# Attention and routed experts: value products in bursts by a fixed table, constants built on the chip, halves swapped by a transfer

## The chip, the cores and the metric

One core of a Trainium2 chip runs the whole program. The metric is the device time of one execution in microseconds; the kernel before is shown with three runs and one profiled execution.

## The reference, cut to what matters

```python
def _attn_ref(q, k, v, tau):                      # q, k, v: (8, 8, 576, 64)
    scores = scale * np.matmul(q, k.transpose(0, 1, 3, 2))
    thresh = np.max(scores, axis=-1, keepdims=True) - tau
    scores = np.where(scores >= thresh, scores, -1000000000.0)
    scores = scores - np.max(scores, axis=-1, keepdims=True)
    attn = np.exp(scores)
    attn = attn / (np.sum(attn, axis=-1, keepdims=True) + 1e-09)
    return np.matmul(attn, v)
def _moe_ref(x, w_gate, w1, w2):                  # x: (4608, 512), 8 experts, F = 1024
    logits = x @ w_gate
    order = np.argsort(-logits.flatten())         # tokens in falling order of their logit,
    ...                                           # each expert takes at most 576
    for e in range(E): out[mask] = np.maximum(x[mask] @ w1[e], 0.0) @ w2[e]
```

## The kernel before, in words

**The attention loop.** Two heads make a pair, four pairs a batch, 32 pairs in all (NP). A pair has nine tiles of 128 queries (the ninth takes the last 64 queries of both heads), so there are NT = 288 tiles, and the loop `for s_ in range(-2,NT//2+2)` (L301) takes two of them in each slot. In slot s, TensorE (PE) issues in this order: the scores of two tiles that are two slots ahead (`score`, L70, into `sc`), a few transposes of leftover columns in some slots (`left`, into free columns of `sc`), value products and other units, and last the 16 transposes of the tiles of this slot (`tr`, L102, into `tb`). VectorE (DVE) does two row minima with a copy (`mx`, L78, the z instructions) and two threshold products (`stt`, L94). ScalarE (ACT) empties `tb` of the slot before (`trev`, L117 and L119, two instructions), takes two exponentials (`ex`, L90), and empties what the slot before has left in the value banks.

**Buffers that tie the engines.** `sc` has two buffers, one for each tile of a slot, so the scores of the next slot wait for the z of this one. `tb` has one buffer for both tiles, so the transposes of a slot wait until ACT has emptied those of the slot before. The value products use two PSUM banks, `xa` and `xb`.

**Value portions.** A pair's value product is nine units: four over the first 256 queries (`pv_unit(p,0,u)`, L154, bank `xa`), four over the other 320 (`pv_unit(p,1,u)`, bank `xb`) and one for the leftover keys (`pl_unit`, L169). One `pv_unit` is two matmuls in the program and four in the trace, since each fp32 matmul is recorded twice. In the kernel before, `push_pair` puts the units into a queue with conditions, and `columns(n=2)` takes two units in each slot as their conditions hold.

**Gates.** When a batch's four pairs are done, `finish` queues its units: two gate products (`lg_unit`, L190), their transposes (`lgt_unit`, L201, `lgm_unit`, L210), and for batches 0 and 1 five units that transpose the rows and store them (`xt_unit`, L222). `whole()` issues one of them in a slot if a bank is free, after the slot's value portions. The first gate product also holds a matmul with `swap` (L192) that brings the reciprocals of the other half of the partitions, which ACT then copies into `rm` (L197).

**Start and end.** Constants come as one array `cst` by a transfer on the POOL queue (`load_cst`, L946); `Router.consts` (L396) makes bf16 and fp32r copies from it on DVE before the first z. After the loop come the rest of the last pair, the gates of the last batch, and a search over thresholds (`R.phase`), with row transposes of the late batches between its steps. `R.prep(0,28)` and `R.compare` prepare that search for seven of eight batches. The expert part follows (`moe`); its order is set by a planner that keeps a model time of DVE, to which every DVE instruction of the router is added (`Vec`).

Of the kernel before, what the change touches and what calls it, by code (L numbers as in the profile page):

```python
# [9 lines left out]
F32 = mybir.dt.float32  # L10
# [12 lines left out]
def attention(ctx, tc, qk, vl, tau, wgd, xrows, xts, Lg, nb_batches, ident, swap, R, after_first):  # L23
# [154 lines left out]
    def rd_calc(b):  # L178
        rd=wk.tile([128,36],F32,name="rd",bufs=XTB+NBO); RD[b]=rd
        G.tensor_scalar(rd,DEN[b],1e-9,None,op0=ALU.add)  # L180
        V.reciprocal(rd,rd)
        rm=wk.tile([128,4,2],F32,name="rm",bufs=XTB+NBO); RD["m",b]=rm
        for h in range(2):
            r=slice(64*h,64*h+64); G.tensor_scalar(rm[r,:,h],rd[r,32:36],1.0,0.0,op0=ALU.mult,op1=ALU.add)
    LT={}
    def lg_unit(b,f):
        if f==0: LT[b]=wk.tile([128,S+D],F32,name="lt",bufs=LTB)
        ps=bank_g(b,[128,512]); q=FQ[f]; n=q.stop-q.start; rd=RD[b]
        for j in range(4):
            T.matmul(ps[32*j:32*j+32,:n],wg[:,j],XT[b][:,j,q],start=True,stop=True,tile_position=(0,32*j))  # L190
        if f==0:
            T.matmul(ps[:,256:260],swap,rd[:,32:36],start=True,stop=True)  # L192
        def ev():
            A.activation(LT[b][:,q],ps[:,:n],AF.Copy)
            if f==1: G.tensor_scalar(LT[b][:,S:],LT[b][:,S-D:S],1.0,0.0,op0=ALU.mult,op1=ALU.add); return
            for h in range(2):
                r=slice(64*h,64*h+64); A.activation(RD["m",b][r,:,1-h],ps[r,256:260],AF.Copy)  # L197
# [20 lines left out]
    def xt_unit(b,c):  # L218
# [7 lines left out]
        def ev():  # L226
            src=RD[b][:,8*c:8*c+8] if c<4 else RD["m",b][0:64].rearrange("p j h -> p (j h)")
            fv=xr[:n,512:XW]; xv=xr[:n,:512].rearrange("p (j d) -> p j d",j=4)
# [11 lines left out]
    queue=[]; aux=[]; later=[]; late=[]; late2=[]; st={"last":-9,"slot":0}  # L240
    def push_pair(p):
        b,j=divmod(p,4)
        def when(n): return lambda: have.get((p,n),1<<30)+HOLD<=st["slot"]
        def units(f): queue.extend(("c",when("t3" if f==0 else "t8"),lambda f=f,u=u: pv_unit(p,f,u),"ab"[f] if u==0 and (f==0 or late_p(p)) else None) for u in range(4))
        def note(w,g): queue.append(("n",w,g,None))
        units(0)
        if j==3: note(when("t8"),lambda: rd_calc(b))
        if p==NP-1:


            units(1)
            def left(f):
                for k,g in pl_unit(p,(f,)): g(); VB[k]["free"]=True
            for g in (lambda: left(0),lambda: left(1),lambda: lg_unit(b,0)(),lambda: lg_unit(b,1)(),lambda: lgt_unit(b)(),lambda: lgm_unit(b)()):
                note(when("pl"),g)
            note(lambda: not later,lambda: late.extend([lambda c=c: xt_unit(b,c) for c in range(5)]))
            return
        queue.append(("c",when("pl"),lambda: pl_unit(p),"b"))
        units(1)
        if (b,j)==(nb_batches-1,2): note(lambda: not aux,lambda: (R.prep(0,28),R.compare(R.k("E1"),J,0,28)))  # L260
        if j==3: note(lambda: not later,lambda: finish(b))
    def finish(b):
        aux.extend([(2,lambda: lg_unit(b,0)),(2,lambda: lg_unit(b,1)),(2,lambda: lgt_unit(b)),(2,lambda: lgm_unit(b))])
        rows=[lambda c=c: xt_unit(b,c) for c in range(5)]
        if nb_batches-NDEF-NBO<=b<nb_batches-NDEF:
            nc.sync.dma_start(xts[b],XT[b]); late2.extend(rows)
        elif b<nb_batches-NDEF: aux.extend([(1,x) for x in rows])
# [6 lines left out]
    def columns(n=2):  # L274
        while queue and queue[0][1]():
            k,_,g,bk=queue[0]
            if k=="c":
                if n==0: return
                if bk and not VB[bk]["free"]: return
                n-=1  # L280
            queue.pop(0); r=g()
            if k=="c" and r: later.extend(r)
# [685 lines left out]
```

## Time and profile before

| what | value |
|---|---|
| median of 3 runs | 991.3 us (991.24 to 991.8) |
| the profiled execution, its own time | 989.73 us |
| its span, first to last instruction | 988.0 us (1.73 us lie around it) |
| mean granted TensorE clock | 0.988 |
| busy: PE, DVE, ACT, POOL | 954.5, 769.8, 641.0, 224.7 us |

A busy PE is not a PE at its peak: the ends of matmuls are modelled, and the time between two starts says more than the length of one. The chain is the work that ended last, followed back from the end. An idle time in brackets stands before the instruction that it delayed.

### The profile page before, as it was taken

Reading aid. Unit: us, or ns where it says so; the run is one execution under the profiler, and the core shown is the slowest. Engines: PE = TensorE matmul, PEld = TensorE weight load, DVE = VectorE, ACT = ScalarE, POOL = GpSimd, SP = SyncE. Lnnn points to the kernel's source line nnn. Section 1 sums busy time; section 2 is a strip of 40 time slices with the busy share of each in tenths; the row PEclk is TensorE's granted clock in tenths of the full one; section 3 lists DMA queues with packets and bytes.
Section 4 is the critical chain, followed back from the end, with each engine's and each line's share of the span. In section 5 each row is a group of like instructions: output and inputs, shape, how many; then the busy total and the mean of one; then the engine's idle time right before and its main releaser. Section 6 shows DMA issues by size and latency. Waiting matters only on the chain.

```text
span 988.0 us, 23677 instructions
## 1 busy us (share of the span) xinstructions
PE 954.5 (97%) x9141; PEld 707.4 (72%) x9141; DVE 769.8 (78%) x2100; ACT 641.0 (65%) x1283; POOL 224.7 (23%) x292
## 2 busy tenths in 40 slices
PE   6999999999999999999779999999999999999996
PEld 3566556555665566555679798897988979898994
DVE  6999999999999999997579878687787786535220
ACT  4999998999999998987645344253452534545340
POOL 2222322323222222222020313221302213310202
PEclk8999999999999999999979999999999999999998
DMA  6233241452432323303760705243433435341101
GB/s 233 96 107 121 103 157 55 169 182 88 169 122 98 121 90 117 121 2 121 268 222 2 245 28 181 93 136 112 141 122 113 145 108 166 100 149 41 38 12 42
DMA packets 35792, 116.97 MB, mean 118 GB/s; under 512 B 4384, under 2 KB 5024, under 8 KB 35168
## 3 DMA queue, kind: packets, MB, share of 16 engines
q1 hardware_dynamic: 28208, 92.58, 27.4%
q0 software_dynamic: 5968, 19.29, 6.2%
q10 hardware_dynamic: 1504, 3.59, 1.2%
q8 instruction: 72, 1.18, 0.5%
q14 instruction: 40, 0.33, 0.1%
HBM read 93.01 MB, written 21.38 MB: 116 GB/s over the span
## 4 chain that ended last, share of the span: by engine, by line
PE 90%; DVE 4%; DMA 2%; issue 2%; ACT 1%; ACTq 0%; POOLq 0%; POOL 0%; DVEq 0%
PE pf L798 21%; PE pf L830 19%; PE sc L70 15%; PE tb L102 9%; PE xb L154 8%; PE xa L154 6%; PE pt L743 2%; PE xa L169 1%; PE rps L451 1%; PE sc L102 1%; DMA out_dram<-y,idx 1%; PE xa L222 1%; DMA cst<-cst_dram 1%; DMA w1s<-w_dram 1%; DVE cmp L383 1%
## 5 line engine op out<-in xcount | busy, mean ns | idle before, releaser
L78 DVE TENSOR_SCALAR_CACHE_REDUCE z<-sc 128x576 f32<-128x576 f32 x288 | 205.6, 750 | 18.0 <-PE sc L70 16.0
L90 ACT ACTIVATE pp<-z,nb 128x576 f32<-128x576 f32 x256 | 193.2, 773 | 32.8 <-DVE z L78 31.1
L94 DVE SCALAR_TENSOR_TENSOR pp<-z,nb,pp 128x576 f32<-128x576 f32 x256 | 199.7, 812 | 0.0
L830 PE MATMUL pf<-w2h,H 128*128 128x512 f32 x576 | 195.1, 402 | 0.7 <-DVE H L383 0.7
L70 PE MATMUL sc<-qk 64*128 64x288 f32 (+1 forms) x1280 | 180.8, 427 | 5.8 <-DVE z L78 5.4
L79 POOL TENSOR_SCALAR nb<-nb,taub 128x2 f32<-128x2 f32 x144 | 105.9, 736 | 320.5 <-ACT pp L90 166.6
L117 ACT ACTIVATE pt<-tb 128x512 f32<-128x512 f32 x256 | 139.3, 590 | 5.3 <-PE tb L102 4.8
L830 PE MATMUL pf<-w2l,H 128*128 128x512 f32 x320 | 128.3, 401 | 0.0
L830 PEld LDWEIGHTS pf<-w2h,H 128*128 128x128 f32 x576 | 106.5, 189 | 19.9 <-DVE H L383 1.5
L70 PEld LDWEIGHTS sc<-qk 64*128 64x128 f32 (+1 forms) x1280 | 94.4, 180 | 35.4 <-DVE z L78 8.7
L102 PEld LDWEIGHTS tb<-ident,pp 64*128 64x128 f32 x2048 | 75.5, 139 | 54.1 <-issue 23.6
L837 POOL DMA_INDIRECT out_dram<-y,idx x40 | 43.8, 1095 | 305.9 <-ACT y L833 239.1
L798 PE MATMUL pf<-xh,w1h 128*128 128x288 f32 (+2 forms) x512 | 110.1, 301 | 0.7 <-ACT xh L744 0.7
L798 PE MATMUL pf<-xl,w1h 128*128 128x288 f32 (+2 forms) x512 | 110.1, 301 | 0.0
L798 PE MATMUL pf<-xh,w1l 128*128 128x288 f32 (+2 forms) x512 | 109.5, 299 | 0.0
L833 ACT ACTIVATE y<-pf 128x512 f32<-128x512 f32 x40 | 23.9, 598 | 127.5 <-PE pf L830 124.1
L102 PE MATMUL tb<-ident,pp 64*128 64x64 f32 x2048 | 94.1, 229 | 2.6 <-ACT pt L117 2.6
L810 ACT ACTIVATE hf<-pf 128x576 f32<-128x576 f32 x56 | 36.5, 653 | 89.5 <-PE pf L798 82.8
L154 PE MATMUL xb<-pt,vt 128*64 128x320 f32 x512 | 86.3, 448 | 0.0
L798 PEld LDWEIGHTS pf<-xh,w1h 128*128 128x128 f32 x512 | 82.0, 190 | 1.5 <-ACT xh L744 1.1
L798 PEld LDWEIGHTS pf<-xl,w1h 128*128 128x128 f32 x512 | 82.0, 190 | 0.0
L798 PEld LDWEIGHTS pf<-xh,w1l 128*128 128x128 f32 x512 | 81.8, 189 | 0.1
(214 smaller groups left out, 1398.4 us busy)
## 6 DMA issues: line engine op xcount, KB each, us to landing
qk<-qk_dram SPq DMA_DIRECT2D x31, 864.0 KB, 4.7
vt<-vl_dram SPq DMA_DIRECT2D x32, 576.0 KB, 3.8
w2s<-w_dram SPq DMA_DIRECT2D x32, 512.0 KB, 4.4
w1s<-w_dram SPq DMA_DIRECT2D x28, 512.0 KB, 5.7
xrows<-pp SPq DMA_DIRECT2D x24, 260.0 KB, 2.2
xts<-xt SPq DMA_DIRECT2D x2, 1152.0 KB, 5.2
pt<-xts SPq DMA_DIRECT2D x2, 1152.0 KB, 7.4
xrows<-xr SPq DMA_DIRECT2D x8, 260.0 KB, 2.4
```

Of the source, the lines that this page charges most:

```text
L70: T.matmul(sc[o,f,:HS], kd["q",h][r,c], kd["k",h][r,:],start=True,stop=True)
L78: V.tensor_scalar(z,SC.pop(t)[:,:,:HS],-0.125,None,op0=ALU.mult,op1=ALU.min,accum_out=nb[:,0,t%2:t%2+1])
L79: G.tensor_scalar(nb[:,1],nb[:,0],taub[:,0:1],None,op0=ALU.add)
L90: A.activation(pview(t),ZB[t].rearrange("p a b -> p (a b)"),AF.Exp,bias=NBI[t][:,0:1],scale=-1.0)
L94: V.scalar_tensor_tensor(pv,ZB.pop(t).rearrange("p a b -> p (a b)"),NBI[t][:,1:2],pv,op0=ALU.is_le,op1=ALU.mult,accum_out=den_of(p)[:,dcol ...
L102: g=slice(64*r,64*r+64); T.transpose(o[:,r],x[r%len(x)][g],ident[g,g])
L117: A.activation(PT[p][:,i%2,:,(i//2)*128:(i//2+1)*128].rearrange("p k (r q) -> p r k q",r=2),tb,AF.Copy)
L154: T.matmul(xo[64*h:64*h+64,:q.stop-q.start],v[:,f,128*u+64*h:128*u+64*h+64],PT[p][:,h,u,q],start=opens,stop=closes,skip_group_check=True)
L798: T.matmul(ps[:,h,:n],s[w][:,k,f*128:(f+1)*128],s[x][:,k,cols[h]],start=(i==0),stop=(i==11))
L810: A.activation(hf,ps[:,:,:HS],AF.Relu)
L830: T.matmul(ps[:,0,:],H[:,f,c:c+128],s[w][:,f],start=(f==0 and j==0),stop=e)
L837: G.indirect_dma_start(out=out,out_offset=IOA(ap=s["idx"][:n,t:t+1],axis=0),in_=y[:n],in_offset=None)
```

## The change

Value portions follow a table: in each round of nine slots (two pairs), slots 4, 6, 8, 1 and 3 (counted modulo 9) get 4, 4, 4, 4 and 2 units, and the others none. The gate condition reads `plan.get(slot)` after `columns()` has taken the slot's entry out. The `swap` matmul and its two ACT copies go; two small transfers on the SP queue bring the other half into `rm`. The `cst` array loses two 128-column parts and is loaded by the SP queue behind the first pairs; POOL makes the triangle with two selections, DVE takes the identity from `ident`, and three copies move to POOL in slot 9 (`consts2`). `R.prep(0,28)` and its compare move from behind the loop into slot 138. The last pair's portions in the last slots and behind the loop are written out.

```diff
 def rd_calc(b):
         G.tensor_scalar(rd,DEN[b],1e-9,None,op0=ALU.add)
-        V.reciprocal(rd,rd)
-        rm=wk.tile([128,4,2],F32,name="rm",bufs=XTB+NBO); RD["m",b]=rm
+    def rd_inv(b):
+        rd=RD[b]; V.reciprocal(rd,rd)
+        rm=wk.tile([128,2,4],F32,name="rm",bufs=XTB+NBO); RD["m",b]=rm.rearrange("p h j -> p j h")
         for h in range(2):
-            r=slice(64*h,64*h+64); G.tensor_scalar(rm[r,:,h],rd[r,32:36],1.0,0.0,op0=ALU.mult,op1=ALU.add)
+            r=slice(64*h,64*h+64); o=slice(64-64*h,128-64*h)
+            G.tensor_scalar(rm[r,h],rd[r,32:36],1.0,0.0,op0=ALU.mult,op1=ALU.add)
+            nc.sync.dma_start(rm[r,1-h],rd[o,32:36])
...
-        if f==0:
-            T.matmul(ps[:,256:260],swap,rd[:,32:36],start=True,stop=True)
...
-            for h in range(2):
-                r=slice(64*h,64*h+64); A.activation(RD["m",b][r,:,1-h],ps[r,256:260],AF.Copy)
...
-    def push_pair(p):
...
+    CYCLE=[(4,((0,0,0),(0,0,1),(0,0,2),(0,0,3))),(6,((0,2,0),(0,1,0),(0,1,1),(0,1,2))),(8,((0,1,3),(1,0,0),(1,0,1),(1,0,2))),
...
+    plan[z-3]=[x for x in plan.get(z-3,[]) if x[0]<NP-1]; plan[z-2]=rest; plan[z-1]=[(NP-1,0,u) for u in range(4)]
...
-    def columns(n=2):
-        while queue and queue[0][1]():
...
+    def columns():
+        for x in plan.pop(st["slot"],()): portion(*x)
     def whole():
-        if aux and st["slot"]>=st["last"]+aux[0][0] and spare():
+        if aux and spare() and (not plan.get(st["slot"]) or aux[0][0]>=nb_batches-2):
...
-    after_first()
+    R.consts(ident)
     load(0)
     if NP>1: load(1)
     nc.sync.dma_start(wg,wgd)
-    R.consts()
+    after_first()
...
+        if s_==9: R.consts2()
...
         columns(); whole()
+        if s_==NT//2-6:
+            while len([x for x in aux if x[0]<nb_batches]): flush(); whole()
+            flush(); R.prep(0,28); R.compare(R.k("E1"),J,0,28)
         for t in tr_: tr(t,t==tr_[0])
...
+    for u in range(4): pv_unit(p,1,u)
+    left(0); left(1)
...
-        s.tri=t("trib",[128,128],BF16); V.scalar_tensor_tensor(s.tri,s.k("eye"),BIGS,s.k("tri"),op0=ALU.mult,op1=ALU.add)
-        s.eye=t("eyer",[128,128],F32R); V.tensor_copy(s.eye,s.k("eye"))
+        G.affine_select(s.tri,s.ones,pattern=[[1,128]],compare_op=ALU.is_gt,fill=0.0,base=0,channel_multiplier=-1)
+        G.affine_select(s.tri,s.tri,pattern=[[1,128]],compare_op=ALU.not_equal,fill=BIGS,base=0,channel_multiplier=-1)
+        s.eye=t("eyer",[128,128],F32R); V.tensor_copy(s.eye,ident)
...
+    def consts2(s):
+        for o,n in ((s.w8,"w8"),(s.ihl[:,0],"ihi"),(s.ihl[:,1],"ilo")): s.G.tensor_scalar(o,s.k(n),1.0,0.0,op0=ALU.mult,op1=ALU.add)
...
-        def load_cst(): nc.gpsimd.dma_start(cst,cst_d)
+        def load_cst(): nc.sync.dma_start(cst,cst_d)
```

PE, slots 132 to 134 (6 to 8 of their round) of the kernel before. `sc<-qk` are scores, `sc<-ident` leftover transposes, `xa` and `xb` value portions (L169 the leftover keys), `tb` the transposes that end a slot; an x8 of portions is four units.

```order
L70 MATMUL sc<-qk 64x288 x4
L169 MATMUL xa<-pl,vt 64x256 x2
L169 MATMUL xb<-pl,vt 64x320 x2
L154 MATMUL xb<-pt,vt 64x320 x2
L102 MATMUL tb<-ident,pp 128x64 x16
L70 MATMUL sc<-qk 128x288 x4
L154 MATMUL xb<-pt,vt 64x320 x4
L102 MATMUL tb<-ident,pp 128x64 x16
L70 MATMUL sc<-qk 128x288 x4
L102 MATMUL sc<-ident,pp 128x64 x6
L154 MATMUL xb<-pt,vt 64x320 x2
L154 MATMUL xa<-pt,vt 64x256 x2
```

The same place in the changed kernel; slots 6 and 8 are bursts, slot 7 has no portion.

```order
L70 MATMUL sc<-qk 64x288 x4
L169 MATMUL xa<-pl,vt 64x256 x2
L169 MATMUL xb<-pl,vt 64x320 x2
L154 MATMUL xb<-pt,vt 64x320 x6
L102 MATMUL tb<-ident,pp 128x64 x16
L70 MATMUL sc<-qk 128x288 x4
L102 MATMUL tb<-ident,pp 128x64 x16
L70 MATMUL sc<-qk 128x288 x4
L102 MATMUL sc<-ident,pp 128x64 x6
L154 MATMUL xb<-pt,vt 64x320 x2
L154 MATMUL xa<-pt,vt 64x256 x6
```

The two units of slot 7 went into slots 6 and 8 on either side of it; in a round with gates, slot 7 gets a gate unit alone.

DVE at the end of the loop before: the preparation of the search (L383) stands behind the last threshold products of the last pair.

```order
L78 TENSOR_SCALAR z,nb<-sc 128x576 x2
L94 SCALAR_TENSOR_TENSOR pp,den<-z,nb,pp 128x576 x3
L94 SCALAR_TENSOR_TENSOR pm_101,den<-z,nb,pm_101 128x576
L383 TENSOR_REDUCE b<-Lg 128x28
L383 TENSOR_TENSOR q<-Lg,b 128x224
L383 TENSOR_TENSOR q<-q,w8b 128x224
L383 TENSOR_REDUCE qm<-q 128x28
L383 TENSOR_TENSOR oh<-q,qm 128x224
L383 TENSOR_TENSOR cmp<-b,cst 128x896
L181 RECIPROCAL rd<-rd 128x36
```

The same six instructions now (L374), in slot 138: three more slots of z follow them.

```order
L94 SCALAR_TENSOR_TENSOR pm_100,den<-z,nb,pm_100 128x576
L94 SCALAR_TENSOR_TENSOR pp,den<-z,nb,pp 128x576
L374 TENSOR_REDUCE b<-Lg 128x28
L374 TENSOR_TENSOR q<-Lg,b 128x224
L374 TENSOR_TENSOR q<-q,w8b 128x224
L374 TENSOR_REDUCE qm<-q 128x28
L374 TENSOR_TENSOR oh<-q,qm 128x224
L374 TENSOR_TENSOR cmp<-b,cst 128x896
L78 TENSOR_SCALAR z,nb<-sc 128x576 x2
L94 SCALAR_TENSOR_TENSOR pp,den<-z,nb,pp 128x576 x2
```

What stood between the attention loop's DVE work and the search now stands inside that work.

## Rows read from the trace of the kernel before

**Rows 1.** The page: its first line, busy time of each engine with its share of the span and its instructions, and the chain that ended last by engine.

```profile
span 988.0 us, 23677 instructions
...
PE 954.5 (97%) x9141; PEld 707.4 (72%) x9141; DVE 769.8 (78%) x2100; ACT 641.0 (65%) x1283; POOL 224.7 (23%) x292
...
PE 90%; DVE 4%; DMA 2%; issue 2%; ACT 1%; ACTq 0%; POOLq 0%; POOL 0%; DVEq 0%
```

**Rows 2.** Busy time of each engine in three stretches of the span (from:to and length in us; then PE, PEld, DVE, ACT, POOL with instructions; granted TensorE clock, DMA share, GB/s): the attention loop, the end of attention with the first search, the experts.

```profile
460.00:507.00 47.00, 36.08 (x405) 27.49 (x401) 26.31 (x85) 26.29 (x71) 6.42 (x7) 0.93 0.73 257
11.00:460.00 449.00, 445.56 (x5358) 266.21 (x5360) 428.17 (x1194) 411.44 (x804) 121.73 (x185) 0.99 0.33 113
507.00:988.00 481.00, 468.89 (x3356) 410.72 (x3355) 311.98 (x797) 201.99 (x407) 93.63 (x90) 0.99 0.33 106
```

**Rows 3.** Timeline of the first 16 us, all engines (start us, us, engine, line, operation, output<-inputs, shapes, count, and in brackets the idle time before it and what ended it).

```profile
1.67 0.43 SPq L45 DMA_DIRECT2D qk<-qk_dram  x1
...
4.12 1.93 PE L70 MATMUL sc<-qk 64*128 64x288 f32 x8
...
8.45 0.29 DVE L383 SCALAR_TENSOR_TENSOR trib<-cst 128x128 bf16<-128x128 f32 x1 [6.30 <-DMA cst<-cst_dram]
...
10.41 0.75 DVE L78 TENSOR_SCALAR_CACHE_REDUCE z<-sc 128x576 f32<-128x576 f32 x1
...
13.56 0.76 DVE L78 TENSOR_SCALAR_CACHE_REDUCE z<-sc 128x576 f32<-128x576 f32 x1 [0.19 <-PE sc L70]
...
15.73 0.75 DVE L78 TENSOR_SCALAR_CACHE_REDUCE z<-sc 128x576 f32<-128x576 f32 x1
```

**Rows 4.** Transfers issued in the first 14 us: line of the second piece of the first pair on the SP queue, with KB and us from issue to landing.

```profile
qk<-qk_dram SPq DMA_DIRECT2D x1, 224.0 KB, 6.2
```

**Rows 5.** The chain that ended last, in order of time (start us, us, what), between 299 and 356 us: pieces of two successive rounds of nine slots, the first with the gates of a batch.

```profile
299.88 1.33 PE sc L70 x12
...
328.48 1.33 PE sc L70 x12
...
343.56 1.03 PE sc L70 x8
344.59 1.23 PE xb L154 x8
...
347.48 0.18 PE sc L102 x6
347.67 0.69 PE xb L154 x4
348.35 0.43 PE xa L154 x4
...
355.18 1.08 PE sc L70 x9
```

**Rows 6.** Timeline around slots 5 to 7, all engines, columns as in rows 3. Slot 5 is one of the few of the program as it stands that has no value portion.

```profile
30.06 0.60 ACT L117 ACTIVATE pt<-tb 128x512 f32<-128x512 f32 x1
...
30.71 0.71 PE L102 MATMUL tb<-ident,pp 64*128 64x64 f32 x16 [0.76 <-ACT pt L117]
...
31.26 0.71 PE L70 MATMUL sc<-qk 64*128 64x288 f32 x4
...
32.16 0.72 PE L70 MATMUL sc<-qk 64*64 64x288 f32 x8 [0.19 <-ACT pl L132]
...
33.34 0.76 PE L154 MATMUL xb<-pt,vt 128*64 128x320 f32 x4
...
34.03 0.72 PE L102 MATMUL tb<-ident,pp 64*128 64x64 f32 x16
...
34.58 1.19 PE L70 MATMUL sc<-qk 64*128 64x288 f32 x8
...
35.57 0.75 DVE L78 TENSOR_SCALAR_CACHE_REDUCE z<-sc 128x576 f32<-128x576 f32 x1
```

**Rows 7.** Timeline of the loop between 270 and 304 us: the first z of two successive slots on DVE.

```profile
283.36 0.75 DVE L78 TENSOR_SCALAR_CACHE_REDUCE z<-sc 128x576 f32<-128x576 f32 x1
...
286.20 0.75 DVE L78 TENSOR_SCALAR_CACHE_REDUCE z<-sc 128x576 f32<-128x576 f32 x1
```

**Rows 8.** Timeline between 307 and 312 us, the slot after a first gate unit: its scores on PE and the z that waited for them.

```profile
309.57 1.19 PE L70 MATMUL sc<-qk 64*128 64x288 f32 x8
...
310.32 0.76 DVE L78 TENSOR_SCALAR_CACHE_REDUCE z<-sc 128x576 f32<-128x576 f32 x1 [0.83 <-PE sc L70]
```

**Rows 9.** Who waited for whom between 11 and 460 us (us in total, times, longest us).

```profile
DVE z L78 <- PE sc L70: 16.0, 26, 0.8
```

**Rows 10.** Timeline of the end of the attention part, columns as in rows 3.

```profile
456.10 0.37 DVE L383 TENSOR_REDUCE b<-Lg 128x28 f32<-128x224 f32 x1
...
457.35 0.46 PE L102 MATMUL tb<-ident,pp 64*128 64x64 f32 x8
...
457.97 1.08 DVE L383 TENSOR_TENSOR cmp<-b,cst 128x896 bf16<-128x896 f32 x1
...
459.46 2.32 PE L154 MATMUL xb<-pt,vt 128*64 128x320 f32 x16
...
462.41 1.05 PE L190 MATMUL sc<-xt,wg 128*32 128x256 f32 x8
...
463.39 0.38 PE L192 MATMUL sc<-rd,swap 128*128 128x4 f32 x2
```

More of the change, by code (lines that the diff above doesn't have):

```diff
@@ L234, in xt_unit @@
         return ev
-    queue=[]; aux=[]; later=[]; late=[]; late2=[]; st={"last":-9,"slot":0}
-    def push_pair(p):
-        b,j=divmod(p,4)
[L243 to L261, printed above, removed]
@@ new lines, in attention @@
+    CYCLE=[(4,((0,0,0),(0,0,1),(0,0,2),(0,0,3))),(6,((0,2,0),(0,1,0),(0,1,1),(0,1,2))),(8,((0,1,3),(1,0,0),(1,0,1),(1,0,2))),
+          (10,((1,0,3),(1,2,0),(1,1,0),(1,1,1))),(12,((1,1,2),(1,1,3)))]
+    plan={}
+    for c in range(NP//2):
+        for o,x in CYCLE:
+            for i,f,u in x: plan.setdefault(9*c+o,[]).append((2*c+i,f,u))
+    for k in range(NT//2-2,NT//2+20): plan.pop(k,None)
+    z=NT//2; seen={x for y in plan.values() for x in y}
+    rest=[x for x in [(NP-2,2,0)]+[(NP-2,1,u) for u in range(4)] if x not in seen]
@@ L262, in finish, with portion @@
+    plan[z-3]=[x for x in plan.get(z-3,[]) if x[0]<NP-1]; plan[z-2]=rest; plan[z-1]=[(NP-1,0,u) for u in range(4)]
+    aux=[]; later=[]; late=[]; late2=[]; st={"last":-9,"slot":0}; soon=[]
+    def portion(p,f,u):
+        b,j=divmod(p,4)
+        r=pl_unit(p) if f==2 else pv_unit(p,f,u)
+        if r: later.extend(r)
+        if f==1 and u==3 and j==3 and p<NP-1: soon.append((1,lambda: finish(b)))
     def finish(b):
-        aux.extend([(2,lambda: lg_unit(b,0)),(2,lambda: lg_unit(b,1)),(2,lambda: lgt_unit(b)),(2,lambda: lgm_unit(b))])
@@ L273, in flush @@
         later.clear()
-    def columns(n=2):
-        while queue and queue[0][1]():
[L276 to L282, printed above, removed]
+    def columns():
+        for x in plan.pop(st["slot"],()): portion(*x)
     def whole():
-        if aux and st["slot"]>=st["last"]+aux[0][0] and spare():
+        if aux and spare() and (not plan.get(st["slot"]) or aux[0][0]>=nb_batches-2):
             before={n for n in "ab" if VB[n]["free"]}
-            r=aux.pop(0)[1](); st["last"]=st["slot"]
+            r=aux.pop(0)[1]()
             later.append((next(iter(before-{n for n in "ab" if VB[n]["free"]}),None),r))
     idle=cst.tile([128,128],BF16,name="idle"); V.memset(idle,0.0)
-    after_first()
+    R.consts(ident)
     load(0)
@@ L305, in attention @@
         for p,n in p8: left(p,n,sc_[-1] if sc_ else None)
+        if s_==9: R.consts2()
         flush()
+        for n,g in [x for x in soon if x[0]<=0]: g()
+        soon[:]=[(n-1,g) for n,g in soon if n>0]
         for t in ev_:
-            p,i=divmod(t,9)
-            while i==0 and p>1 and (p-2,"pv") not in have: columns(9); flush()
-            trev(t); have[p,f"t{i}"]=s_
-        if ev_ and ev_[-1]==NT-1: columns(9)
-        for t in ev_:
-            p,i=divmod(t,9)
-            if i==3: push_pair(p)
-            if i==8: have[p,"pl"]=s_
+            p,i=divmod(t,9); b=p//4
+            trev(t)
+            if i==8 and p%4==3: rd_calc(b); soon.append((0,lambda b=b: rd_inv(b)))
         mx(sc_)
@@ L325, in attention, with left @@
         columns(); whole()
+        if s_==NT//2-6:
+            while len([x for x in aux if x[0]<nb_batches]): flush(); whole()
+            flush(); R.prep(0,28); R.compare(R.k("E1"),J,0,28)
         for t in tr_: tr(t,t==tr_[0])
-    st["slot"]+=9
-    while queue or aux or later:
-        st["slot"]+=1; flush(); columns(9); whole()
+    flush()
+    for n,g in soon: g()
+    p=NP-1; b=p//4
+    def left(f):
+        for k,g in pl_unit(p,(f,)): g(); VB[k]["free"]=True
+    for u in range(4): pv_unit(p,1,u)
+    left(0); left(1)
+    for g in (lambda: lg_unit(b,0),lambda: lg_unit(b,1),lambda: lgt_unit(b),lambda: lgm_unit(b)): g()()
+    late.extend([lambda c=c,b=b: xt_unit(b,c) for c in range(5)])
     for k in range(0,NBO,2):
```

26 lines of the change are left out of this document (13 added, 13 removed).

## The prediction

> **What bounds the kernel now.** I read the page first. PE is busy 97% of the span, DVE 78%, and 90% of the chain that ended last is PE [rows 1]. By stage: the loop takes 449 us, in which PE shows 445.6 us, DVE 428.2 and ACT 411.4; the experts take 481 us and the change does not name them [rows 2]. So in the loop three engines stand within 8% of each other, and what matters is which one waits where. In the chain [rows 5] the loop is PE alone, back to back: scores 1.03 us, eight portion matmuls 1.23, and so on. Two rounds of nine slots take 55.3 us (28.6 from 299.88 to 328.48 with the gates of a batch, 26.7 from there to 355.18 without). DVE, left alone, needs 2.84 us for a slot [rows 7], 51.1 for 18, and over the loop its busy time is 428.2/8 = 53.5 for 18. So PE is ahead of DVE as the bound by under 2 us in 55, and DVE's waits for scores add up to only 16.0 us in 26 waits, 2.0 per 18 slots [rows 9]. The first microseconds are another case: DVE stands 6.30 us until `cst` lands and the first z starts at 10.41, though the first scores were begun at 4.12 [rows 3].
>
> **The start.** Without the load, DVE makes its constants from `ident` while the first pair is still on its way. The copies took 8.45 to 10.41, 1.96 us with those that now go; begun at some 2 us they end near 4, before the first scores are there at about 5. The first two z then come 4 to 5 us earlier. The third tile needs another piece of the queries: issued at 1.67, landed 6.2 later, 7.9 [rows 3, 4]. I put the third z at about 8.6 and the fourth at 9.4, where the fourth stood at 13.56, so everything behind moves by 4.2 us. Bounds: 3.4 (the two pairs of scores keep the 1.93 us that eight matmuls take here) to 5.3 (the piece lands earlier, since `cst` no longer travels beside it). POOL gets two selections, covered since it only feeds sums needed after the first z; SP issues `cst` behind the pairs, and the next load has several slots to spare. The sum takes **-4.2**.
>
> **What a burst saves.** A unit of four recorded 320-column matmuls costs 0.69 us at the head of a block, while the next unit in the same block, four of 256 columns, costs 0.43 [rows 5]. Eight of 320 cost 1.23, so one is (1.23-0.69)/4 = 0.135 and the block's fixed part is 0.69-0.54 = 0.15; with the entry that the score piece carries in front, up to 0.26. Rounds without gates go from nine blocks to five, but a leftover unit in the middle of slot 1's block costs one more change: 0.26x4-0.15 = 0.9 us saved per such round, in the best case. Rounds with gates go from five to nine blocks again, since each gate unit now stands alone in slot 5, 7, 0 or 2; they keep only the `swap` matmul, 0.32 us. So PE's own sum falls by about 1.05 us per 18 slots, 6.8 us over the loop after the extra blocks of the row units in batches 0 and 1. By the Trainium skill (TensorEngine Tiling (Array Packing), Key Properties), changing the tiling mode drains the TensorE; the fixed part of a block is what the trace shows of it, and by that rule alone the loop would be 6.8 us shorter, which is a rival below.
>
> **What a burst costs.** PE can't run ahead in an empty slot. The program has a few already, at its start: in slot 5 the transposes wait 0.76 us for ACT's copy out of `tb` and start at 30.71, the scores of slot 6 at 31.26, the second of them held until 32.16 by ACT's copy of leftovers; then the leftover unit, four portion matmuls, transposes at 34.03, scores of slot 7 at 34.58, and z at 35.57, exactly when DVE is ready [rows 6]. A z can start 0.75 us after the first score of its slot (309.57 to 310.32) [rows 8]. Now put twelve matmuls where four were: 8x0.135 = 1.08 later, scores at 35.66, z at 36.41, and DVE waits **0.84 us**. That is one burst.
>
> I carried this through two rounds by three rules from rows: scores of a slot start when z has read the bank, z 0.75 after them, transposes when ACT is done with the slot before, each slot's own work from rows 5. For the kernel before this gives 55.1 us where the rows show 55.3. For the changed one PE's work outside the scores and transposes is 2.15, 2.4, 2.25 and 2.55 us in slots 4, 6, 8 and 1, 1.33 in slot 3, and none or a gate in the rest (a leftover unit is about 0.65 of it, what lies between 32.16 and 33.34 beyond its slot's second scores [rows 6]). DVE waits four times in 18 slots, 0.99, 0.86, 0.49 and 0.86, and PE itself loses 2.7 us in empty slots where it lost nothing. Two rounds come to 55.9: **+0.8**. Four such pairs of rounds give +3.2; the two with row units come out 1.1 shorter each (PE had the most to do there), -2.2; the first two rounds, where DVE hardly waited before, are 1.9 longer together, and the last slots 0.3. The loop: **+3.2**. Bounds: -6.8 (only the saving) and +5.3 (a change between scores and transposes costs 0.1 us in an empty slot too, which no row excludes, since no row has them back to back with PE as the bound).
>
> **The preparation of the search.** It runs from 456.10 to 459.05 on DVE, at a time when nothing waits for it [rows 10]. In slot 138 it stands in front of the z of slot 139, with DVE the engine that is waited for: **+3.0**, at least +2 if PE still has some lag to give.
>
> **The tail.** Before, the last transposes start at 457.35 and a block of 12 portion matmuls covers ACT's last copies; the second portions begin at 459.46 and the gates at 462.41 [rows 10]. Now four units, 16x0.107 = 1.7 us, stand ahead of the last transposes instead of two, and slot 141 has three units instead of one. Last transposes +1.4 later against the last z, then no cover: the second portions wait for ACT 1.85 us after them, where it was 2.11. Together +1.2, less the 0.32 of `swap` on this path: **+0.9**. ACT's two `rm` copies go with it. The transfers for `rm` have several slots; nothing waits for them.
>
> **The experts.** No instruction is new, but DVE's model time in the planner has fewer constants in it, so the order shifts in places. I take 0, within 2 us either way.
>
> **Sum.** -4.2+3.2+3.0+0.9 = **+2.9 us**. On the profiled execution's own 989.73 (span 988.0 and 1.73 around it) that is 992.6. The median of the runs lies 1.6 above that execution, so the forecast is 991.3+2.9 = **994.2 us**. The measurement of this kernel can tell about 0.2%, 2 us, from no change.
>
> **Rivals.**
> - *Bursts are hidden* (the other sign). If ACT is earlier than I have it in the empty slots, PE's scores come in time, DVE never waits longer than now, and the drains saved remain: -4.2-6.8+2+0.9 = -8.1, 983.2. For it: PE is the bound in every piece of the chain. The rule on drains in the Trainium skill (TensorEngine Tiling (Array Packing), Key Properties) points this way. Against it: rows 6 show the wait of the transposes in empty slots, and DVE has no slack for 6.8 us plus the preparation. It decides at the z behind slots 6 and 1: with no wait over 0.3 us there, this one holds. Chance 0.15.
> - *Bursts cost nothing and save nothing*: the loop at 0, so -0.3, 991.0; likely somewhere between -2 and +2. Chance 0.25.
> - *More is lost*: +5.3 in the loop and 1.5 in the expert order, +6.5, 997.8. In a slot with a gate alone, the unit pays its entry and delays the scores of the next burst. Chance 0.18.
> - *The change doesn't do what it says at the start*: the constants are built in time, but the second pair of scores waits so long for its piece that only 1 us is won: 997.4. Against it: that piece lands at 7.9 even beside `cst`. Chance 0.07. The gate condition does nothing in most batches, since the slot's entry is already taken out; the order puts the gates into empty slots all the same, so that has no price.
> - The forecast itself: 0.35.
>
> **How the numbers follow.** Above 993.3 (slower by over 0.2%) lie most of the forecast's case, the third and the fourth rival: 0.30+0.18+0.06 = 0.54. Below 989.3 lie the first rival, and the lower edge of the second: 0.15+0.06 = 0.21. The rest is 0.25. The range leaves out 1 in 10 on each side: 984.5, inside the first rival, to 999.0, past the third; the likeliest case alone reaches from 992 to 997.
>
> **What would show it.** The first z near 5.5 us and the fourth near 9.4. In the loop: z waits for scores of 0.5 to 1.0 us behind slots 6, 8 and 1, in sum a few us over the 16.0 of before; transposes that wait for ACT in slots 0 and 5; chain pieces by DVE in the loop. The six L374 instructions with a gap of 3 us between two z. The gates of the last batch begin 1.2 us later against the last z than before. Wrong would be a loop shorter than the 449 us of before, counted from the fourth z, with no new waits (then the first rival holds), or an end of attention that does not move against the last z.

## The result and the profile after

The changed kernel takes **1003.9 us** (median; 1001.3 to 1004.8), the kernel before 991.3 beside it: 1.0126 times as long, 95% interval 1.0114 to 1.0138. The forecast was 994.2, in a range up to 999.0. The sign was right, the size was not: +12.6 us where +2.9 was forecast. The profiled execution is the lowest of the four (1001.3, span 999.6), so the trace has 11.6 us to explain.

The page, against [rows 1]:

```profile
span 999.6 us, 23669 instructions
...
PE 953.7 (95%) x9125; PEld 707.5 (71%) x9125; DVE 766.8 (77%) x2096; ACT 637.5 (64%) x1267; POOL 233.7 (23%) x296
...
PE 46%; DVE 2%; DMA 1%; issue 0%; ACT 0%; POOLq 0%; DVEq 0%; ACTq 0%
```

PE's share fell from 97% to 95%, although the program has no more work for it. The chain adds up to half the span only: it was not followed back into the loop. So the loop has to be read by its own clock, the first z of each pair of tiles. Below, "pair" with a number means such a pair of tiles, the two tiles of one slot (0 to 143), and not two heads. "To pair 138" means from the first z (pair 0) to the first z of pair 138; the expectations call this slot 0 to slot 138. Slots of nine are the loop's own, as in the table of the diff; a pair's z come two slots before its transposes.

The start (timeline, DVE), against [rows 3]:

```profile
5.54 0.76 DVE L78 TENSOR_SCALAR_CACHE_REDUCE z<-sc 128x576 f32<-128x576 f32 x1 [1.88 <-PE sc L70]
...
7.88 0.76 DVE L78 TENSOR_SCALAR_CACHE_REDUCE z<-sc 128x576 f32<-128x576 f32 x1 [0.89 <-PE sc L70]
...
8.56 0.75 DVE L78 TENSOR_SCALAR_CACHE_REDUCE z<-sc 128x576 f32<-128x576 f32 x1
...
10.72 0.75 DVE L78 TENSOR_SCALAR_CACHE_REDUCE z<-sc 128x576 f32<-128x576 f32 x1
```

The first z was forecast at about 5.5 and the fourth at 9.4, and they stand at 5.54 and 8.56; the fifth moved from 15.73 to 10.72. The start works.

Busy time of the loop to pair 138 and of 18 slots in it (from pair 90 to pair 108), kernel before, then after (columns: stretch, length, busy PE, PEld, DVE, ACT, POOL, granted clock, DMA share, GB/s):

```profile
10.41:437.19 426.78, 422.75 (x5074) 252.81 (x5076) 406.78 (x1136) 391.39 (x764) 115.51 (x176) 0.99 0.35 118
289.03:344.15 55.12, 55.12 (x671) 32.94 (x671) 53.14 (x151) 51.17 (x102) 15.26 (x22) 1.00 0.32 107
```

```profile
5.54:443.16 437.62, 423.83 (x5072) 254.00 (x5072) 405.18 (x1134) 388.34 (x750) 121.04 (x179) 1.00 0.34 120
290.98:347.76 56.78, 55.38 (x671) 33.11 (x669) 53.10 (x150) 50.58 (x100) 17.03 (x22) 1.00 0.30 106
```

The loop to pair 138 is 10.84 us longer. PE was busy in all 55.12 us of the 18 slots before; now it shows 55.38, no less, and stands idle for 1.40 besides (busy PE can hold waits, as shown below). Who waited for whom from 6 to 475 us (us, times, longest), against [rows 9]:

```profile
DVE z L78 <- PE sc L70: 32.9, 37, 1.9
...
PEld tb L102 <- ACT pt L117: 28.8, 52, 1.5
...
PEld sc L70 <- ACT pl L132: 14.9, 31, 0.6
...
PE tb L102 <- ACT pt L117: 7.8, 17, 1.0
```

Before, over the same stretch, these rows had 16.0, 10.6, 3.2 and 2.6. In the 18 slots from 290.9 us alone, DVE's row is

```profile
DVE z L78 <- PE sc L70: 3.6, 5, 1.2
```

An empty slot (0 of nine) and the burst behind it, on the timeline of all engines:

```profile
295.96 1.19 PE L70 MATMUL sc<-qk 64*128 64x288 f32 x8
...
296.41 0.43 ACT L160 ACTIVATE xt<-xb 128x320 f32<-128x320 f32 x1
...
297.20 0.61 ACT L119 ACTIVATE pt<-tb 128x512 f32<-128x512 f32 x1
...
297.87 0.71 PE L102 MATMUL tb<-ident,pp 64*128 64x64 f32 x16 [0.60 <-ACT pt L119]
...
298.41 1.50 PE L70 MATMUL sc<-qk 64*128 64x288 f32 x8
298.65 0.45 ACT L132 ACTIVATE pl<-sc 64x64 f32<-64x64 f32 x2
...
299.15 0.30 PEld L70 LDWEIGHTS sc<-qk 64*128 64x128 f32 x4 [0.49 <-ACT pl L132]
...
301.12 1.30 PE L154 MATMUL xb<-pt,vt 128*64 128x320 f32 x8
...
302.35 0.71 PE L102 MATMUL tb<-ident,pp 64*128 64x64 f32 x16
...
302.99 1.40 PE L70 MATMUL sc<-qk 64*64 64x288 f32 x12
303.78 0.76 DVE L78 TENSOR_SCALAR_CACHE_REDUCE z<-sc 128x576 f32<-128x576 f32 x1 [1.07 <-PE sc L70]
```

PE stands 0.60 us until ACT has emptied `tb`, then again until ACT has copied leftovers out of the bank of the second scores (299.15), then has four portions to do, and DVE waits 1.07 us for the scores behind them. The second of these waits hardly shows as idle PE: the eight scores from 298.41 on show 1.50 us busy, where the eight from 295.96 on show 1.19. So a longer busy time of PE is not more work.

The preparation (timeline, DVE): the first z of pairs 140 and 141, and the piece between them.

```profile
449.50 0.74 DVE L78 TENSOR_SCALAR_CACHE_REDUCE z<-sc 128x576 f32<-128x576 f32 x1
...
452.33 0.37 DVE L374 TENSOR_REDUCE b<-Lg 128x28 f32<-128x224 f32 x1
...
454.20 1.08 DVE L374 TENSOR_TENSOR cmp<-b,cst 128x896 bf16<-128x896 f32 x1
455.20 0.75 DVE L78 TENSOR_SCALAR_CACHE_REDUCE z<-sc 128x576 f32<-128x576 f32 x1
```

These 5.70 us were 2.82 before. Behind the loop (timeline, PE), against [rows 10]:

```profile
469.74 2.37 PE L154 MATMUL xb<-pt,vt 128*64 128x320 f32 x16 [1.05 <-ACT pt L119]
...
472.74 1.59 PE L193 MATMUL sc<-xt,wg 128*32 128x256 f32 x16
474.33 0.97 PE L200 MATMUL sc<-ident,lt 128*128 128x128 f32 x4
...
503.25 0.21 PE L524 MATMUL rps<-gq,trib 128*128 128x72 bf16 x1 [0.70 <-DVE gq L374]
...
512.32 0.39 PE L446 MATMUL rps<-oh,cmp 128*128 128x32 bf16 x9 [1.15 <-DVE cmp L374]
...
517.27 1.94 PE L738 MATMUL pt<-ident,xg 128*128 128x128 f32 x8 [3.99 <-DVE jka L374]
519.90 1.23 PE L793 MATMUL pf<-xh,w1h 128*128 128x256 f32 x4 [0.69 <-ACT xh L739]
```

**The sum, measured** on the two traces: start -4.87 (first z), loop to pair 138 +10.84, from there to pair 143 +3.11 (2.88 of it the preparation), pair 143 to the gates +1.25, the gates without `swap` -0.54, from their transposes to the first expert matmul +2.31, experts -0.50: +11.6.

### The profile page after: what moved, and what is told of

It is laid out like the page before. It is cut to its first block, busy times and chain, and to the rows that moved or that the text cites. A ratio compares the mean times of both kernels' runs of the same rounds, so it can differ in the third digit from the quotient of the medians.

```text
span 999.6 us, 23669 instructions
## 1 busy us (share of the span) xinstructions
PE 953.7 (95%) x9125; PEld 707.5 (71%) x9125; DVE 766.8 (77%) x2096; ACT 637.5 (64%) x1267; POOL 233.7 (23%) x296
## 5 line engine op out<-in xcount | busy, mean ns | idle before, releaser
L70 PE MATMUL sc<-qk 64*128 64x288 f32 (+1 forms) x1280 | 184.6, 427 | 5.0 <-DVE z L78 3.2
L79 POOL TENSOR_SCALAR nb<-nb,taub 128x2 f32<-128x2 f32 x144 | 109.7, 762 | 323.6 <-ACT pp L90 175.8
L70 PEld LDWEIGHTS sc<-qk 64*128 64x128 f32 (+1 forms) x1280 | 91.3, 178 | 41.8 <-ACT pl L132 14.9
L832 POOL DMA_INDIRECT out_dram<-y,idx x40 | 46.7, 1168 | 312.3 <-ACT y L828 210.6
L805 ACT ACTIVATE hf<-pf 128x576 f32<-128x576 f32 x56 | 36.6, 653 | 89.9 <-PE pf L793 83.3
L154 PE MATMUL xb<-pt,vt 128*64 128x320 f32 x512 | 82.8, 445 | 1.1 <-ACT pt L119 1.1
```

The costliest lines, as they stand in the source:

```text
L70: T.matmul(sc[o,f,:HS], kd["q",h][r,c], kd["k",h][r,:],start=True,stop=True)
L79: G.tensor_scalar(nb[:,1],nb[:,0],taub[:,0:1],None,op0=ALU.add)
L154: T.matmul(xo[64*h:64*h+64,:q.stop-q.start],v[:,f,128*u+64*h:128*u+64*h+64],PT[p][:,h,u,q],start=opens,stop=closes,skip_group_check=True)
L805: A.activation(hf,ps[:,:,:HS],AF.Relu)
L832: G.indirect_dma_start(out=out,out_offset=IOA(ap=s["idx"][:n,t:t+1],axis=0),in_=y[:n],in_offset=None)
```

## Experiments

**1. The parts by themselves.** The start alone (constants, loads and their order of the diff put into the kernel before; `swap` and the order of the portions as before):

```diff
-    after_first(); load(0); ...; R.consts()
+    R.consts(ident); load(0); ...; after_first()
```

> The kernel before with only the start of the change (constants from the identity, their load behind the queries'). The first z moves from 10.41 to 5.54 us and the second pair's stt from 15.73 to 10.72 in the changed kernel, and nothing else differs. Theory that the start is worth all of this and the loss lies in the loop: 991.3-5.0 = 986.3 us, with every later slot as long as before. Rival, that most of the start is given back later because DVE only runs into PE sooner (the first rounds are then the longer): 989 or more, and the 18 slots from slot 0 on are 2 us or more longer than before.

986.9 us, ratio 0.996 (0.9947 to 0.9973). First z at 5.64; the loop to pair 138 takes 426.44 us for 426.78. So what the start wins is kept, as expected (986.3). With the halves swapped by transfer too (the hunks on `rd_inv`, `lg_unit` and `xt_unit`):

> As the one with only the start, and the halves swapped by transfer instead of by matmul, still two portions a slot. The swap's matmul is 0.32 us of PE in each of eight batches, two copies of ACT go with it. Theory that it is hidden in the loop but for the last batch: 986.3-0.3 = 986.0 us. Rival, that the gates now wait for the two transfers (each about 2 us): about 1 to 2 us slower than with the start alone, with gates' DVE work late.

985.1 us, 0.9942 (0.9929 to 0.9954). The loop is 0.89 us shorter again and the gates 0.54, more than the -0.3 expected; no gate waits for the transfers. The matmul was not hidden in the loop, as the theory had it: from pair 18 to pair 138 the loop takes 373.24 us for 375.42, 0.31 less in each of seven rounds with gates, while the first nine slots of this trace took 1.3 longer. Both are faster than the kernel before: what costs is the rest.

The preparation put back behind the loop (`R.prep(0,28); R.compare(...)` after the last slot):

> The changed kernel with the preparation of the search put back behind the loop. In the changed kernel the slot that holds it lasts 5.70 us where the others of its kind last 2.83 to 2.96. Theory that it stands wholly in DVE's way: 2.9 us less than the changed kernel, 1003.9-2.9 = 1001.0. Rival, that in its slot PE gets ahead and the time comes back in the next slots or in the tail: less than 1 us gained.

998.9 us, 1.0079 (1.0066 to 1.0092). By medians that is 5 us less, by the traces less so: pair 9 to pair 143 takes 426.57 us for 429.47, 2.90 less, as expected; before pair 9 this trace lost 1.05 us with the same instructions. What the rest of the 5 us is stays open.

**2. The same table, made even.**

```diff
-    CYCLE=[(4,(4 portions)),(6,(4)),(8,(4)),(10,(4)),(12,(2))]
+    CYCLE=[(4+k,tuple(SEQ[2*k:2*k+2])) for k in range(9)]   # same order
```

> The changed kernel with its table alone made even: the same 18 portions in the same order, two in each of the nine slots instead of four in four and two in one. Start, preparation, gates' rule and tail stay as changed. Theory that the empty slots cost the 11 us of the loop (PE can't run ahead in them, its transposes wait for ACT and its scores for the leftovers' copies): the loop falls to about the time of before, 1003.9-10 = 994 us within 2, the z's waits for scores fall from 32.9 us to under 18, and the transposes' for ACT from 36.6 to under 20. Rival, that a fixed table costs it whatever its filling (gates and row units stand where they stand): 1001 to 1004, with the waits as they are.

990.1 us, 0.9991 (0.998 to 1.0002), with the preparation still in DVE's way. To pair 138 it takes 424.37 us: the bursts alone cost **13.25**, of which 10.84 lie behind pair 18 (that the whole loop grew by 10.84 over the kernel before is another sum). The windows and waits of this kernel:

```profile
5.59:429.96 424.37, 419.82 (x5064) 249.75 (x5064) 407.60 (x1133) 390.42 (x750) 116.32 (x179) 1.00 0.35 123
282.77:337.57 54.80, 54.80 (x669) 32.63 (x669) 53.22 (x152) 50.99 (x100) 15.24 (x22) 1.00 0.31 109
```

```profile
DVE z L78 <- PE sc L70: 15.6, 31, 1.9
...
PEld tb L102 <- ACT pt L117: 10.2, 16, 1.5
```

PE is busy without a gap here, as in the kernel before. From pair 18 to pair 138 it takes 373.16 us, the kernel with start and swap alone, with its queue, 373.24. A fixed table is not the trouble; its filling is.

**3. Which feature of the filling?** Four tables with the same order (portions in slots 4 to 12): 3,1,3,1,3,1,3,1,2; the changed one a slot later; one lone empty slot, 0 of nine (2,2,2,2,4,0,2,2,2) or 7 of nine (2,2,4,0,2,2,2,2,2).

> The changed kernel with its table as 3,1,3,1,3,1,3,1,2 portions: the bursts stay, one portion longer than two a slot, but no slot is empty. Read from slot 0 to slot 138, where the changed kernel takes 437.6 us and the even table 424.4 (13.2 apart). Theory that the empty slots do it (nothing stands on PE between the scores and the transposes, so the transposes wait for ACT): most of the 13.2 comes back, 425 to 428 us, whole time 991 to 994. Rival, that the length of a burst does it (scores behind it come late, z waits): half of it stays, 430 to 432, whole time 996 to 998.

> The changed kernel with the whole table one slot later, so that the bursts fall in slots 5, 7, 0, 2 and 4 of nine and the empty slots in 6, 8, 1 and 3. The slots in which ACT copies the second leftovers out (the two kinds of slot with 4.1 us of ACT work) then hold a burst, and were empty. Theory that the empty slots cost what they cost because of ACT's extra copies there: the loop to slot 138 falls from 437.6 to 430 or less. Theory that any empty slot costs the same, wherever it is: 437 within 2. Rival of both, that the portions now come a slot too late for the buffers: over 440.

> The even table (two portions in each slot) with one pair of portions of 18 put a slot earlier: slot 8 of nine has four, slot 0 none. Slot 0 is one in which ACT also copies leftovers out. There are 16 such places, and all four of a cycle together cost 13.2 us from slot 0 to slot 138. Theory of ACT's extra copies: this one and its like carry it, so 5 to 7 us here, 429.5 to 431.5 us to slot 138. Theory that every empty slot costs the same: 3.3 us, 427.7. Rival that only whole patterns cost (a lone empty slot is taken up by the slots around it): under 1.5 us, below 426.

> As the one before, but slot 6 of nine has four portions and slot 7 none; in slot 7 ACT has no leftovers to copy. Theory of ACT's extra copies: under 1.5 us against the even table, 424.4 to 426 us to slot 138. Theory that every empty slot costs the same: 3.3 us, 427.7. Rival that a lone empty slot is taken up: under 1.5 us as well, so that this run tells the first from the second only together with the one before.

Lengths to pair 138, and from pair 18 (the first 18 slots differ by 1 us between runs of one and the same order, 53.62 and 54.67):

```
table          0 to 138   18 to 138   over even   whole time
even           424.37     373.16      -           990.1
3,1,3,1,...    429.67     377.57      +4.4        994.4
empty slot 7   429.60     376.05      +2.9        994.8
empty slot 0   432.94     380.62      +7.5        999.4
the change     437.62     384.00      +10.8       1003.9
one slot later 437.75     384.36      +11.2       1004.2
```

No theory came through whole. Without empty slots 3,1 still loses 4.4 us. Both lone empty slots cost more than was expected of them (432.94 for 429.5 to 431.5; 429.60 for at most 427.7). The slot with ACT's leftover copies is the dear one (7.5 against 2.9; the two make nearly all of 10.8, but the empty slots 2 and 5 were not tried alone, so how the four add up is not shown). The table one slot later took the 437 of the theory that every empty slot costs the same, which these two runs contradict. Moving the bursts into just those slots won nothing, and other waits are there: transposes for ACT's `pt` stand at 32.1 us there, scores for the first leftover copy at 13.7 (1.0 before the move).

**4. Taking the waits away one by one**, each in the changed and in the even table. First ACT's copies out of `tb`, cut to a quarter (POOL fills the rest with zeros):

```diff
-  A.activation(PT[p][:,i%2,:,c]...,tb,AF.Copy)
+  A.activation(PT[p][:,i%2,:1,c]...,tb[:,:,:1],AF.Copy); G.memset(PT[p][:,i%2,1:,c],0.0)
```

> The changed kernel in which ACT copies only the first quarter of each transposed tile out of tb; the other three quarters of pt are filled with zeros by POOL (the portions are computed from zeros there). An ACT copy of 512 columns takes 0.59 us and one of 256 takes 0.37, so a copy of 128 is estimated at 0.27 and ACT has about 0.64 us less to do in each slot. Only the loop is read, against the even table with the same cut. Theory that the transposes' wait for ACT's copies in the empty slots is the loss: the 13.2 us between the two tables to slot 138 shrink to 4 or less. Rival, that the loss is the uneven work itself (a slot with four portions is longer than DVE's 2.84 us, and in an empty slot PE can get no further ahead than two score banks allow, whatever ACT does): 9 us or more remain.

> The even table with the same cut of ACT's copies, for comparison. In it PE is busy for all of 54.8 us of 18 slots and ACT is not waited for, so both theories expect little: 422 to 424.5 us to slot 138, where the even table takes 424.4.

Then DVE's threshold pass too (`h=slice(0,144)` on its operands), then the leftovers (`left` issues nothing, `leftev` is a fill of `pl` by POOL), and at last the leftovers alone:

> The changed kernel with ACT's copies cut to a quarter as before, and DVE's threshold pass (stt) cut to 144 of its 576 columns as well (the other columns keep their exponentials). DVE's 2.84 us of a slot are estimated to fall to about 1.9 (two z of 0.68 and two passes of about 0.27, worked out from 0.74 for 576 columns and a fixed part as in the smaller passes of the rows). Only the loop is read, against the even table with the same two cuts. Theory that the table costs time because DVE has no slack to take a burst (a slot with four portions keeps it waiting, and in the empty slot it can't go faster than 2.84): with DVE at 1.9 PE makes up in the empty slot what it loses in the burst, and the gap to slot 138 falls from 12.05 us to 4 or less. Rival, that bursts cost PE itself (its own work is longer, or it can't start the next scores early whatever DVE does): 8 us or more remain.

> The even table with the same two cuts, for comparison. PE is busy throughout in it, 54.8 us of 18 slots, so a faster DVE is worth little: 417 to 425 us to slot 138 where it is 425.3 with the copies cut alone. Rival, that DVE's pass is the bound here as well: under 412.

> The changed kernel with both cuts of the runs before (ACT's copies to a quarter, DVE's pass to 144 columns) and without the leftovers: PE doesn't transpose them into the score banks, ACT doesn't copy them out, POOL fills pl with zeros instead. With that no score waits for a leftover's copy (22.3 and 5.0 us of waits in the run with both cuts). Only the loop is read, against the even table with the same cuts. Theory that a table's cost is the sum of whatever PE waits for in the empty slots, one wait behind the other, and that this is the last of them: the gap to slot 138 falls from 11.1 us to 4 or less. Rival, that bursts cost time by PE's own work (its blocks take longer in bursts, whatever it waits for): 8 us or more remain.

> The even table with the same three cuts, for comparison. PE has some 0.5 us less to do in each of four slots of 18, so the loop to slot 138 falls from 420.8 us by about 15, to 402 to 410, if PE alone bounds it; 416 or more if something else has become the bound.

> The changed kernel without the leftovers alone (no transposes of them into the score banks, no copies of them by ACT, pl filled with zeros by POOL); ACT's copies out of tb and DVE's pass are whole again. Only the loop is read, against the even table with the same cut. With all three cut the gap to slot 138 was -2.2 us, with the two others cut 11.1. Theory that the leftovers in the score banks alone carry the burst's cost: 3 us or less remain here. Theory of a row of interchangeable waits: with the leftovers gone ACT's copies or DVE's want of slack hold PE instead, and 5 to 10 us remain.

> The even table with the same one cut, for comparison: PE has some 2 us of 54.8 less to do in 18 slots and DVE 53.2 as before, so 412 to 420 us to slot 138, with DVE and PE both near the bound.

```
taken away                    bursts  even    gap     gap from pair 18
nothing                       437.62  424.37  +13.25  +10.84
ACT's copies                  437.35  425.30  +12.05   +9.65
ACT's copies, DVE's pass      431.97  420.84  +11.13   +7.11
these and the leftovers       409.68  411.92   -2.24   -3.24
the leftovers alone           427.17  417.89   +9.28   +6.07
```

The last column is the one to read, since the first 18 slots scatter. The even table with the copies cut took 425.30, over the 422 to 424.5 expected, all of it there: from pair 18 on it takes 373.12 us, uncut 373.16.

With the copies cut, the wait that the forecast rested on shrinks to a fifth, and the next one has grown (waits of the changed table with the copies cut; L118 is its `pt` copy, L134 its leftover copy):

```profile
DVE z L78 <- PE sc L70: 33.4, 43, 1.9
...
PEld sc L70 <- ACT pl L134: 17.7, 31, 1.0
...
PEld tb L102 <- ACT pt L118: 5.3, 11, 0.8
...
PE tb L102 <- ACT pt L118: 2.1, 6, 0.4
```

With the pass cut as well, the scores' wait for leftover copies is 22.3 us. The 11.1 us of the gap that remain are in the range of the rival, that bursts cost time by PE's own work; the run with all three gone speaks against it. With the leftovers alone gone, transposes wait for ACT's copies as before, and scores for z instead (15.6, in the changed kernel 9.4):

```profile
PEld tb L102 <- ACT pt L117: 30.5, 52, 1.5
...
PEld sc L70 <- DVE z L78: 15.6, 36, 2.1
```

Of the four combinations tried, only the one with all three gone leaves PE no idle time. Which two of them would do is not tried, nor DVE's pass alone. Windows of 18 slots (pair 90 to 108) with all three gone, changed table, then even:

```profile
272.97:326.48 53.51, 53.51 (x631) 31.16 (x629) 37.56 (x149) 37.40 (x82) 22.21 (x62) 1.00 0.32 112
```

```profile
273.81:327.61 53.80, 53.80 (x631) 30.24 (x629) 38.34 (x150) 37.52 (x82) 21.89 (x62) 1.00 0.31 112
```

PE is busy in all of both, and now the bursts save: 0.29 us in these 18 slots, 3.24 from pair 18 to pair 138. Where the rest of the saving went shows in the time from one start on PE to the next, summed from pair 18 to pair 138 (the first two columns whole, the others with all three gone):

```
from                      even    bursts    even, gone  bursts, gone
score to next score       99.4    105.2     99.3        102.9
score to anything else    33.8     34.3     38.5         36.8
leftover transposes       13.1     19.6      -            -
portions, gates, rows    159.7    157.6    159.6        155.0
tb transposes             67.2     67.3     67.2         66.7
sum                      373.2    384.0    364.7        361.4
```

In the whole kernels the bursts cost 5.9 us between scores and 6.5 behind leftover transposes, where PE's next instruction waits, and save 2.1 in the portions. With all three gone everything but the steps between scores is 6.8 us shorter; those are 3.5 longer, and scores still wait there for z:

```profile
PEld sc L70 <- DVE z L78: 13.4, 33, 1.8
```

In the even table with all three gone that row has 5.1. The table 3,1 loses its 4.4 us in another way: 2.0 between scores and 2.6 in portions, gates and rows, so it is no clean test of a burst's length.

The expectation of a row of interchangeable waits holds (5 to 10 us were expected to remain without the leftovers alone; 9.3 did, 6.1 from pair 18 on). In the even table the first two cuts won 3.5 us (424.37 to 420.84), nearly all of it in the first 18 slots (51.21 to 48.16): with DVE busy for 38.38 us instead of 53.22, 18 slots in the middle took 54.99 us for 54.80. So PE is its bound there. The leftovers won it 8.9 us more, less than the 11 to 19 expected.

**5. Behind the loop.** The planner's model time set as before (`R.V.free+=0.7167`), and the version to which the runs point: even table, preparation behind the loop, two portions less ahead of the last transposes, that model time.

> The changed kernel with the planner's model time for DVE set to what it was before the change (0.717 us more at the end of attention), which gives the matmuls from the search on the order they had before; the loop is untouched. From the first transposes of the last gates to the first matmul of the first expert 43.3 us passed before, 45.6 in the changed kernel, of which 0.95 is the search and 1.8 the wait for the first gathered rows. Theory that the planner's order makes both: 43.3 again, 2.3 us less than the changed kernel, 1001.6. Rival, that the wait for the rows comes from other transfers in flight: only the 0.95 comes back.

> The even table with the preparation of the search behind the loop, two instead of four portions ahead of the last transposes, and the planner's model time as before: what the runs so far point to. To slot 138 424.4 us as the even table; last z to the gates 10.6 as before, where the even table has 11.8; gates to first expert as in the run beside it. Together 985.1 (the start and the swap alone) less 1.1 of the loop and 2.3 behind it: 981.7 us. Rival, that the wait for the gathered rows stays: 983.5.

The first took 1001.2 us (1.0116, 1.0092 to 1.014): the search is 28.01 us again (before 27.98, changed 28.92). The wait for the first gathered rows (from the last comparison's matmuls to the first transposes of `xg`; 3.17 before, 4.95 changed) was 2.88 here but 4.52 in the second kernel with the same model time. What moves it stays open. The second took **985.0 us**, 0.9937 (0.9922 to 0.9952), the fastest with the start and the swap alone (985.1): its loop is 1.1 us shorter, the search 0.9, the tail 0.3 longer. It missed the 981.7 expected and, by its median, the rival's 983.5. Of the 1.1 us of the loop 1.0 lie in the first nine slots, where equal orders differ by as much, so the even table and the rest bring nothing measured beyond the start and the swap.

## Why the prediction was wrong

- **Start**: -4.2 forecast, -4.87 at the first z, -5.11 at pair 138 with the start alone. Right, a little small: the piece for the third tile landed 5.2 us after its issue, not 6.2 [rows 4], the case that the forecast's upper bound names, and the third z stands at 7.88, not 8.6.
- **What a burst saves**: PE's own sum was to fall by 1.05 us in 18 slots (the two terms named there, 0.9 and 0.32, would make 1.2). Busy PE did not fall, 55.38 us where it was 55.12, because it holds waits. By the times from one start to the next the saving is there: the portions, gates and rows of pair 72 to pair 108, two pairs of rounds, take 1.56 us less than before, 0.8 for each pair (0.3 of it the swap). The price of a block was about right too. In 18 slots of the even table the next start comes 0.33 us after that of a score if a portion follows, 0.24 if a leftover transpose does (64*128 like the scores, where portions are 128*64); it comes 0.36 after that of a portion into `xb` if transposes follow, 0.26 if a portion into `xa` does (medians). That is some 0.1 us at each end of a block, 0.2 in all. The forecast used 0.26, of which [rows 5] give 0.15 and no run shows the rest. The rule of the Trainium skill that a change of tiling mode drains TensorE (TensorEngine Tiling (Array Packing), Key Properties) agrees with these steps.
- **What a burst costs**: this is the step that failed, the +0.8 for a pair of rounds. Its parts were nearly right. z waits behind slots 6, 8 and 1 as forecast: 0.76 and 1.20, 0.42, 1.07 and 0.15 us in 18 slots, 3.6 in sum where 0.99, 0.86, 0.49 and 0.86 make 3.2. PE was to lose 2.7 us in a pair of rounds; by the starts the steps of scores and transposes take 2.4 more. But the sum does not follow from these parts. PE's loss of 2.7 less its saving of 1.05 is +1.65, and DVE's 53.5 us with waits of 3.2 make 56.7, +1.4 over the 55.3 of before; the prediction carried 55.9 and +0.8 on. Measured are +1.65: pair 72 to pair 108, two pairs of rounds, took 113.93 us, before 110.63. That this is the +1.65 of the parts to the digit is luck. In the 18 slots from pair 90 DVE's 53.10 us and its waits of 3.60 fill 56.70 of 56.78.
- **Rounds with row units**: the second part of the same step, forecast 1.1 shorter for each pair of rounds, because PE had most to do there. Pair 27 to pair 63 took 117.89, before 116.42: +1.5 where -2.2 was forecast. Portions, gates and rows took 0.3 us less there, scores and transposes 1.7 more: a saving without waits was forecast, and the waits came there as well.
- **The loop's sum**: +3.2 forecast, +10.84 measured. It is +6.6 for four pairs of rounds (pair 63 to 135; 3.2 forecast), +1.5 with row units (-2.2), +3.2 up to pair 27 (1.9 for the first two rounds, which alone took 2.2 more, with 1 us of scatter), and -0.4 in the last three slots (0.3).
- **The reason given** (transposes wait for ACT in empty slots) was a wait that is there and is not by itself the cause: cut to a fifth, it left 12.05 of 13.25 us. PE had no slack to lose, and by the rows of waits it is held in and behind an empty slot by one of three: ACT's copies out of `tb`, ACT's copies of leftovers, z on DVE. Each of the smaller cuts left more than half of the loss (6.1 to 9.7 of 10.84 us from pair 18 on).
- **Preparation** +3.0: +2.88 in its slot, 2.90 when put back. **Tail** +0.9: +1.25-0.54 = +0.7. Both right.
- **Experts** 0 within 2: -0.5 for the experts, but +2.3 between gates and experts (search +0.94, less 0.41 behind it, rows +1.78), together +1.8, at the edge of the bound. The search's part is the planner's order, as shown; the rows' wait is not settled.
- **Rivals**: "bursts are hidden" was wrong here, though the saving that it counts on, 6.8 us in the loop, is there once the waits are gone (6.8 outside the steps between scores, without the swap; the same figure by chance). "More is lost" had the sign, and half the size.

## What to carry to other kernels

Where an engine is busy in all of a stretch, count each wait that a change puts on it as time lost; work heaped in one slot is not repaid by an empty one, unless what the engine waits for in the empty slot is ready early. Close the sum by each engine: the busy time of the one that waits plus its waits must give the length, and so must the work of the bound engine less what it saves plus what it loses. And before blaming the wait that the trace names, ask which wait stands behind it: removing the first one may only rename the stall.

## What was not expected of the hardware

A wait can vanish from the rows and leave the time as it was: 36.6 us of transposes behind ACT's copies went to 7.4, and the loop moved by 0.3. A weight load that waits can show as longer busy time of PE (1.50 us for eight scores, else 1.19), so PE's busy time rose although its work fell. Equal orders differed by 1 us in the first nine slots (25.86 and 26.91), and by 0.02 or less in later rounds of nine; the first gathered rows were waited for between 2.9 and 5.6 us in the kernels of these runs. The first nine slots and that wait are no evidence for an edit in a single trace.
